# Attention and gated feed-forward on one core: TensorE's order from a written-out plan, and tanh tiles in a ring of eight gate pairs

## The chip, the core and the metric

The kernel runs on one core of a Trainium2 chip. The metric is the device time of one execution in microseconds (us); where several executions were timed, the median stands first and the range behind it. Four compute engines matter: TensorE (PE, matrix products), VectorE (DVE), ScalarE (ACT) and GpSimd (POOL). SyncE (SP) issues DMA transposes here, and GpSimd issues loads and stores. In the traces here each engine takes its instructions in the order of its stream: a copy on ScalarE whose input was complete at 328.97 us starts only at 329.69, behind two tanhs (shown below). The profile also gives the clock that TensorE was granted, as a share of full speed.

## The reference

```python
def _attn_ref(x, inducing):                  # x (4, 12416, 128), inducing (32, 128)
    ...
    def mab(q, kv):
        s = scale * (q @ kv.transpose(0, 2, 1))
        ...                                  # softmax: a
        return a @ kv
    h = mab(I, x)                            # 32 rows for each batch
    return mab(x, h)

def _moe_ref(x, w_gate, w_val, w_out):       # 49664 tokens, d_model 128, d_ff 1536
    gate = 1.0 / (1.0 + np.exp(-(x @ w_gate)))
    val = x @ w_val
    return gate * val @ w_out
```

The second attention multiplies weights `a` (tokens x 32) with `h` (32 x 128), and the feed-forward part multiplies that with `w_gate` and `w_val`. The kernel forms `h @ w_gate` and `h @ w_val` once for each batch, so gate and value need only a product over 32 rows for each token. The sigmoid is (1 + tanh(g/2))/2; the half is applied at the output.

## The kernel before

After a first stage (attention of batch 0) the work is 96 blocks of 512 tokens and a last, mixed one. `d_ff` is 12 chunks of 128. A block has four steps; each step multiplies a wide slot (two chunks, PSUM slot `a`) and a narrow slot (one chunk, PSUM slot `b`) on DVE. ScalarE makes tanh of gate *pairs* (two chunks), TensorE fills the slots and adds up the 12 output products in one PSUM tile, `acc`.

```python
    # buffers
    ps_g ... bufs=2   # gate pairs, and jobs      ps_a, ps_b ... bufs=1   # value slots
    ps_o ... bufs=1   # acc
    tp = ctx.enter_context(tc.tile_pool(name="tp", bufs=2))     # tanh: two whole blocks
    ...
    def g_tanh(bi, p, ps):
        if p == 0:
            Ts[bi] = tp.tile([P, NJ, TOK], F16, tag="T", name=f"T_{bi}")
        nc.scalar.activation(out=Ts[bi][:, 2 * p:2 * p + 2, 0:T], in_=..., func=AF.Tanh, scale=0.5)

    def v_mul(ps, bi, j0, n):                                   # (tanh + 1) * value
        u = up.tile([P, n, TOK], F16, tag=f"u{n}", name=f"u_{bi}_{j0}")
        nc.vector.scalar_tensor_tensor(
            out=u[:, :, 0:T], in0=Ts[bi][:, j0:j0 + n, 0:T], scalar=1.0, in1=...,
            op0=ALU.add, op1=ALU.mult)
        ...

    def out_store(bi):
        ...
        nc.scalar.activation(out=oT[:], in_=accs[bi][:], func=AF.Copy, scale=0.5)   # frees acc
        nc.sync.dma_start(on[:], oT[:], transpose=True)
        nc.gpsimd.dma_start(out[...], on[:])

    # the loop that sets the order
    for n in range(NBK):
        for k in range(4):
            for f in ev.get((n, k), ()):     # loads, transposes, sums of this half step
                f()
            ...
            v_fill(ps, n, 3 * k, 2)          # wide values
            for _ in range(min(pairs, gwant - gdone)):
                g_next()                     # gate pair right behind them
            ua = v_mul(ps, n, 3 * k, 2)
            outs(c0)                         # output matmuls of earlier chunks
            v_fill(ps, n, 3 * k + 2, 1)      # narrow value
            if k == 2 and n in extra:
                post = do_extra(*extra[n])   # a job; the step then does one output matmul less
            elif gdone < gwant:
                g_next(k == 3)
            ub = v_mul(ps, n, 3 * k + 2, 1)
            outs(c1)
```

Meanwhile the next batch's first attention is prepared in *jobs*, one in each of 49 blocks: `s1` (scores of x against the inducing rows, read from `xT`, a DMA transpose of a loaded quarter `xq`), `h` (sums with the exponentials `a1n`, again through a DMA transpose) and others. Where the loads and transposes stand is a table in half blocks:

```python
            plan = (   # load, load, transpose, transpose, s1 job, transpose of the exponentials, h jobs
                ((1, 0), (2, 0), (2, 2), (3, 2), 4, (5, 2), (7, 9)),
                ((5, 0), (6, 0), (6, 2), (7, 2), 8, (9, 2), (12, 13)),
                ((8, 0), (9, 0), (9, 3), (10, 2), 11, (12, 2), (14, 15)),
            )
```

The softmax here doesn't subtract the row's maximum and nothing guards it: scores larger than these inputs give would overflow.

## Time and profile before

| | before |
|---|---|
| time, median (range) | 746.33 us (743.2 to 750.3), 3 runs |
| span of the profiled execution | 739.6 us, granted clock 0.996 |
| busy: PE / DVE / ACT | 654.1 / 705.9 / 646.0 us |
| first to last multiply on DVE | 29.79 to 733.84 us |
| time in it in which DVE does nothing | 9.7 us |

How to read it: DVE is the full engine, so the time can only change by what DVE does or by how long it stands idle. I call "gaps" the time from the start of one DVE instruction to the start of the next, less the 1.14 us (wide) or 0.62 us (narrow) that it needs. The chain that ended last says the same: it is made mostly of DVE, with some TensorE. Shares of the span by engine, before:

```profile
DVE 61%; PE 24%; DMA 6%; ACT 5%; issue 3%; SPq 1%; POOL 0%; ACTq 0%; DVEq 0%; POOLq 0%
```

### The profile page before, as it was taken

The page shows a single profiled execution, that of the slowest core. Times are in us where ns is not written, and L with a number is a line of the kernel's source. Part 1 is how long each engine was busy: PE and PEld are TensorE (multiplying, and loading weights), DVE is VectorE, ACT ScalarE, POOL GpSimd, SP SyncE. Part 2 cuts the span into 40 slices and gives each one's busy share as a digit, 9 for nine tenths or more (in the row PEclk, how much of TensorE's full clock was granted, in tenths as well). Part 3 has the DMA queues.
Part 4 walks back from the last instruction along what each step waited for, and adds up shares of the span by engine and source line. Part 5 has one row for each costly group of instructions (what it writes and reads, how often), then busy time and mean ns, then how long its engine had stood idle before and what let it go on. Part 6 is the DMA issues. An engine that isn't in the chain of part 4 may idle for free.

```text
span 739.6 us, 12305 instructions
## 1 busy us (share of the span) xinstructions
PE 654.1 (88%) x4561; PEld 240.0 (32%) x4561; DVE 705.9 (95%) x838; ACT 646.0 (87%) x727; POOL 210.0 (28%) x317
## 2 busy tenths in 40 slices
PE   7888999989889889989889899998988988888886
PEld 4422333333232333333333233333323333233234
DVE  2599999999999999999999999999999999999997
ACT  4698899899889989889889899989988998988985
POOL 5234314303412512501611511430440241250000
PEclk9999999999999999999999999999999999999999
DMA  9569995523549799532448799562352343253222
GB/s 177 86 98 159 198 193 113 108 57 77 109 75 165 135 184 173 106 74 59 93 94 136 106 200 183 114 116 48 74 106 59 79 92 79 65 106 59 64 58 59
DMA packets 181900, 80.12 MB, mean 108 GB/s; under 512 B 165424, under 2 KB 166096, under 8 KB 181840
## 3 DMA queue, kind: packets, MB, share of 16 engines
q1 hardware_dynamic: 161856, 40.18, 32.9%
q0 software_dynamic: 19696, 39.03, 24.6%
q8 instruction: 35, 0.57, 0.3%
q14 instruction: 25, 0.20, 0.1%
q10 hardware_dynamic: 288, 0.13, 0.1%
HBM read 27.80 MB, written 25.43 MB: 72 GB/s over the span
## 4 chain that ended last, share of the span: by engine, by line
DVE 61%; PE 24%; DMA 6%; ACT 5%; issue 3%; SPq 1%; POOL 0%; ACTq 0%; DVEq 0%; POOLq 0%
DMA xq_4_127<-in_x_dram 2%; DMA xT_151<-xq_1_5310 1%; DMA xT_149<-xq_1_849 1%; DMA xT_149<-xq_3_1228 1%; ACT T_5362 L430 1%; DMA xT_151<-xq_3_5688 1%; DMA xT_150<-xq_3_3458 1%; ACT T_654 L430 1%; ACT T_3590 L430 0%; ACT T_8031 L430 0%; ACT T_7940 L430 0%; SPq L294 0%; ACT T_5820 L430 0%; ACT xT_148 L514 0%; PE acc_694 L472 0%
## 5 line engine op out<-in xcount | busy, mean ns | idle before, releaser
L472 PEld LDWEIGHTS <-wo_112 128*128 128x128 f16 x1152 | 103.4, 96 | 151.7 <-issue 80.8
L375 PEld LDWEIGHTS <-hw_163 32*128 32x128 f16 x432 | 16.5, 91 | 59.9 <-issue 56.9
L375 PEld LDWEIGHTS <-hw_160 32*128 32x128 f16 x434 | 16.4, 91 | 54.4 <-issue 51.0
L375 PEld LDWEIGHTS <-hw_161 32*128 32x128 f16 x432 | 16.3, 91 | 51.7 <-issue 48.2
L375 PEld LDWEIGHTS <-hw_162 32*128 32x128 f16 x432 | 16.2, 91 | 51.7 <-issue 48.2
L375 PEld LDWEIGHTS <-hwp_165 128*128 128x128 f16 x144 | 14.0, 97 | 21.3 <-issue 16.0
L375 PEld LDWEIGHTS <-hwp_166 128*128 128x128 f16 x144 | 13.9, 97 | 21.3 <-issue 15.6
L375 PEld LDWEIGHTS <-hwp_164 128*128 128x128 f16 x142 | 13.8, 97 | 20.9 <-issue 15.3
L375 PEld LDWEIGHTS <-hwp_167 128*128 128x128 f16 x144 | 13.9, 97 | 19.9 <-issue 14.3
L203 PEld LDWEIGHTS <-ones 128*128 128x128 f16 x96 | 7.0, 96 | 5.2 <-issue 3.5
L148 PE MATMUL warm<-ones 128*128 128x512 f16 x16 | 6.0, 558 | 1.5 <-DVE ones L98 1.5
L197 ACT ACTIVATE a1nt_200<-s1t_198 128x32 f16<-128x32 f32 x1 | 0.2, 197 | 6.3 <-PE s1t_198 L193 6.3
L691 PEld LDWEIGHTS <-indT 128*32 128x32 f16 x72 | 1.5, 93 | 9.9 <-issue 9.9
L483 ACT ACTIVATE o_9543<-acc_9458 128x256 f32<-128x256 f32 x2 | 0.8, 383 | 4.4 <-PE acc_9458 L462 3.9
L525 DVE COPY indT<-indT 128x32 f16<-128x32 f16 x1 | 0.2, 175 | 4.6 <-PE indT L524 4.6
L148 PEld LDWEIGHTS <-ones 128*128 128x128 f16 x23 | 2.7, 127 | 5.2 <-issue 3.0
L268 POOL COPY hwp_164<-hw_160 32x128 f16<-32x128 f16 x2 | 0.6, 283 | 13.3 <-ACT hw_160 L261 13.3
L329 POOL TENSOR_TENSOR a_0_2_0_1890<-e2n_2_1725,rc_2_1888 128x512 f16<-128x512 f16 x4 | 4.1, 1037 | 0.7 <-DVE rc_2_1888 L319 0.7
L329 POOL TENSOR_TENSOR a_2_2_0_6350<-e2n_2_6185,rc_2_6348 128x512 f16<-128x512 f16 x4 | 4.1, 1036 | 0.8 <-DVE rc_2_6348 L319 0.8
L329 POOL TENSOR_TENSOR a_1_2_0_4120<-e2n_2_3955,rc_2_4118 128x512 f16<-128x512 f16 x4 | 4.1, 1036 | 0.7 <-DVE rc_2_4118 L319 0.7
L329 POOL TENSOR_TENSOR a_3_1_0_7780<-e2n_1_7649,rc_1_7778 128x512 f16<-128x512 f16 x4 | 4.1, 1037 | 0.5 <-DVE rc_1_7778 L319 0.5
L329 POOL TENSOR_TENSOR a_2_0_0_4880<-e2n_0_4749,rc_0_4878 128x512 f16<-128x512 f16 x4 | 4.1, 1036 | 0.5 <-DVE rc_0_4878 L319 0.5
(4143 smaller groups left out, 2691.4 us busy)
## 6 DMA issues: line engine op xcount, KB each, us to landing
xq_0_115<-in_x_dram POOLq DMA_DIRECT2D x1, 512.0 KB, 5.2
xq_1_117<-in_x_dram POOLq DMA_DIRECT2D x1, 512.0 KB, 7.0
xq_2_123<-in_x_dram POOLq DMA_DIRECT2D x1, 512.0 KB, 8.4
xq_3_125<-in_x_dram POOLq DMA_DIRECT2D x1, 512.0 KB, 10.3
xq_4_127<-in_x_dram POOLq DMA_DIRECT2D x1, 512.0 KB, 13.9
xq_5_129<-in_x_dram POOLq DMA_DIRECT2D x2, 256.0 KB, 14.3
xq_0_758<-in_x_dram POOLq DMA_DIRECT2D x1, 512.0 KB, 6.8
xq_1_849<-in_x_dram POOLq DMA_DIRECT2D x1, 512.0 KB, 6.4
```

Source lines behind the costliest of these rows:

```text
L148: nc.tensor.matmul(ps[:, 0:TOK], ones[:, 0:P], ones[:], start=True, stop=True)
L197: nc.scalar.activation(out=an[:], in_=ps[:, 0:M], func=AF.Exp, scale=SCALE)
L203: nc.tensor.matmul(ps[:, cs:cs + P], ones[:, 0:P], a1n[(b, q)][:, j, :], start=first and j == 0, stop=last and j == 3,)
L268: nc.gpsimd.tensor_copy(out=pads[b][rows, 2 * i + jj, :], in_=hws[b][rows, p, :])
L329: nc.gpsimd.tensor_tensor(out=a2[:, r], in0=e2n[:, i, :, r, :].unsqueeze(2).to_broadcast((P, 4, 4, M)), in1=rc[:, i, :, r].unsqueeze(2).un ...
L375: nc.tensor.matmul(ps[:, ds(col, TOK)], weights(k["b"]), rep[rows, 4 * k["i"] + k["r"]], start=True, stop=True,)
L430: nc.scalar.activation(out=Ts[bi][:, 2 * p:2 * p + 2, 0:T], in_=ps[:].rearrange("p (a t) -> p a t", a=2)[:, :, 0:T], func=AF.Tanh, scale=0.5,)
L472: nc.tensor.matmul(accs[bi][:, 0:T], wo16[:, j, :], u, start=(c == 0), stop=(c == NJ - 1))
L483: nc.scalar.activation(out=o32[:, h:h + w, :].rearrange("p b c -> p (b c)"), in_=accs[bi][:, ds(h * P, w * P)], func=AF.Copy, scale=0.5,)
L525: nc.vector.tensor_copy(out=indT[:], in_=v[:, 0:M])
L691: nc.tensor.matmul(ps[r * M:(r + 1) * M, ts(i, TOK)], indT[:], xTs[a[0]][:, ds(q * QT + r * TOK, TOK)], start=True, stop=True,)
```

## The change

The intent is that TensorE's order is written out, letter by letter, instead of following from a loop. In a word of the plan (one word is a block) `A` fills and multiplies the wide slot of the next step, `B` the narrow one, `G` or `W` fills the next gate pair (`W` with weights that are padded with zeros to all 128 rows), `J` is the next job, and `a` to `l` are output matmuls. The tanh tiles become single pairs in a ring of eight. In odd steps the wide slot takes the last two of its three chunks and the narrow slot the first, so that a wide multiply reads exactly one pair. `PADV` names the chunks whose value weights are padded in the same way; it follows the new order of chunks. A block's store is issued when the next block has had six of its output matmuls.

```diff
+PLAN = (
+    "GAGBWGAabGBcGAfeGBdGAhBWgJ AGilkjBGGAabcBGAfGBedGAhGgBiG ..."
+    ...                                     # 97 words
-    tp = ctx.enter_context(tc.tile_pool(name="tp", bufs=2))
+    tp = ctx.enter_context(tc.tile_pool(name="tp", bufs=8))
-    PADG, PADV = (2,), (2, 5, 8, 11)
+    PADG, PADV = (2,), (2, 3, 8, 9)
 ...
-        if p == 0:
-            Ts[bi] = tp.tile([P, NJ, TOK], F16, tag="T", name=f"T_{bi}")
+        Ts[(bi, p)] = tp.tile([P, 2, TOK], F16, tag="T", name=f"T_{bi}_{p}")
 ...
-        nc.gpsimd.dma_start(out[...], on[:])
+        def store():
+            nc.gpsimd.dma_start(out[...], on[:])
+        stores.append(store)
 ...
+    def chunks(k):
+        return (3 * k, 3 * k + 2) if k % 2 == 0 else (3 * k + 1, 3 * k)
 ...                                         # the loop over n, k is replaced by:
+    for n, word in enumerate(words):
+        for c in word:
+            if c == "A":
+                ...                          # events of the step; v_fill and v_mul, wide
+            elif c == "B":
+                ...                          # v_fill and v_mul, narrow
+            elif c in "GW":
+                next_slot(c == "W")
+            elif c == "J":
+                post = do_extra(*jobs.popleft()[1])
+                if post:
+                    post()
+            else:
+                out_one(cur, ord(c) - ord("a"))
```

(A path that multiplies on GpSimd is in the diff too, but it is never taken.)

## The prediction

> **What bounds the kernel now.** I began with the page's busy shares.
>
> ```profile
> PE 654.1 (88%) x4561; PEld 240.0 (32%) x4561; DVE 705.9 (95%) x838; ACT 646.0 (87%) x727; POOL 210.0 (28%) x317
> ```
>
> The span is 739.6 us. VectorE (DVE) is busy for 705.9 of them, TensorE (PE) and ScalarE (ACT) for under 90%. The slices show that it is one stage and not an average over several.
>
> ```profile
> DVE  2599999999999999999999999999999999999997
> ACT  4698899899889989889889899989988998988985
> POOL 5234314303412512501611511430440241250000
> PEclk9999999999999999999999999999999999999999
> ```
>
> DVE is full from the third slice to the last but one. So the question is how much of its time is not work. I listed all DVE instructions in order of time; this is one block of 512 tokens from the middle.
>
> ```profile
> 346.30 1.22 DVE L443 SCALAR_TENSOR_TENSOR u_0_4734<-T_4686,va_0_4727 128x1024 f16<-128x1024 f16 x1
> 347.44 0.68 DVE L443 SCALAR_TENSOR_TENSOR u_2_4740<-T_4686,vb_0_4738 128x512 f16<-128x512 f16 x1
> 348.05 1.22 DVE L443 SCALAR_TENSOR_TENSOR u_3_4762<-T_4686,va_1_4751 128x1024 f16<-128x1024 f16 x1
> 349.19 0.68 DVE L443 SCALAR_TENSOR_TENSOR u_5_4766<-T_4686,vb_1_4764 128x512 f16<-128x512 f16 x1
> ```
>
> Columns: start, duration, engine, line. Durations overlap by 0.06 to 0.08 us, so I use start to start: 1.14 us from a wide multiply (two chunks of d_ff) to the next, 0.62 us from a narrow one (one chunk). A step is one of each, 1.76 us; a block is four steps, 7.04 us. There are 96 full blocks and a mixed one of the same shape: 388 wide and 388 narrow multiplies. The first starts at 29.79, the last at 733.84, 704.05 us apart. 388 x 1.14 + 387 x 0.62 = 682.2 us of that is multiplies. The excess over these pitches, added over the whole list (with 0.1 to 0.5 us allowed after each small DVE operation, as its own closest follower shows), is 9.7 us; the other 12 us are the small operations themselves. Before 29.79 lies the first attention stage, after the last multiply the output tail of 5.7 us.
>
> Of the 9.7 us, 2.3 lie in block 0 and at the start of block 1. About 4.8 lie behind the nine "s1" jobs (scores of the next batch), which sit in TensorE's in-order stream and wait for a DMA transpose of x. The worst:
>
> ```profile
> PE s_2_3702 L691 <- DMA xT_150<-xq_3_3458: 1.4, 1, 1.4
> PE s_3_5552 L691 <- DMA xT_151<-xq_1_5310: 1.0, 1, 1.0
> PE s_1_1092 L691 <- DMA xT_149<-xq_1_849: 1.0, 1, 1.0
> PE s_3_5932 L691 <- DMA xT_151<-xq_3_5688: 0.8, 1, 0.8
> ```
>
> This is the view of TensorE's waits (total, times, longest, in us). While it stands there it fills no value slot and DVE starves; after the first of these DVE begins its next multiply 1.6 us late, at 271.01. The remaining 2.6 us are lags of under 0.1 us, mostly at a block's first multiply.
>
> **What the Trainium skill says.** "Perfetto Trace Analysis", section Identifying the Most-Contended Engine, takes occupancy as a fair measure for VectorE, but not matmul busy time for TensorE: I trust the 95% and not the 88%. "VectorE: DVE Perf Modes", section Why PSUM operands drop a tier, caps an fp32 PSUM operand at the plain mode of one element a cycle; at the 0.96 GHz of its Specifications 1024 elements are 1.07 us (an estimate from that page) and the trace has 1.14, so the multiply has no slack. Its section The DRAIN you can't avoid found that a semaphore between DVE operations costs nothing extra; here the narrow multiplies with one kind of wait start on average 1.134 us after the wide ones, those with two 1.139, so it agrees. "TensorE: Matmul & The Clock Gate", section The mechanism (packing), says that matmuls on different row groups overlap. The trace agrees: a value pair (rows 64 to 127) and the gate pair after it (rows 0 to 63) start 0.01 us apart, 347.57 and 347.58.
>
> **The change part by part.** I compared the two programs instruction by instruction. TensorE has 9112 of them in both, DVE 840, ScalarE 731, GpSimd 254 and SyncE 172. Nothing is removed or added: the GpSimd multiply path in the diff is dead, because the set of shared blocks is empty. DVE's 388 + 388 multiplies keep their shapes. So 682 + 12 us of DVE work stay, and only the 9.7 us of gaps, the head and the tail can move.
>
> (1) Chunk order in odd steps. A wide multiply now takes exactly one gate pair. Same count and width: 0 us. It lets tanh tiles be rings of pairs.
>
> (2) Ring of eight pairs instead of two whole blocks. Counting the plan, at the first multiply of a step 6 or 7 gate pairs have been issued beyond the one needed (300 of 388 steps), where the old loop ran about 3 or 4 ahead. That takes ScalarE's latency off the path, but in the old trace DVE waited for a tanh only 1.0 us, once, at the very start. Worth under 0.5 us. More multiplies now carry a ScalarE wait: 0 us by the semaphore numbers above.
>
> (3) TensorE order. Before, the gate pair stood right behind the value pair and ran beside it. In the plan the token ahead of a value pair is a gate pair in 320 of 388 steps, and what follows it is mostly output matmuls. Matmuls of 512 columns go every 0.215 us, and each change between row-packed and full matmuls costs about 0.1 us (308.88 to 309.21 for two packed pairs). A block is 12 output matmuls, 4 full value ones, 2 full gate ones, 4 value pairs and 5 packed gate pairs. If each pair runs alone that is 27 x 0.215 = 5.8 us, and with some 12 changes 7.0 us, against 7.04 on DVE. Where the value pair needs not wait, gate and value overlap and it is nearer 6 us. So TensorE stays barely below DVE. Before, a packed value pair had waited for DVE by 0.2 to 0.4 us in many steps; the margin shrinks but I expect it to hold. The small lags are 2.6 us: I take off 1.5.
>
> (4) The head. The plan interleaves gates, values and the first query job at block 0's end. The 2.3 us may shrink to about 1, but the job now stands directly before the DVE reduction that reads it, which can cost some 0.7 again: take off 1.
>
> (5) Jobs and stores. The s1 job moves from the third step of its block to the second, about 1.8 us earlier, for all nine. Alone that would deepen the six waits in the first two rounds by as much: +8 or more. Against it, the HBM store of a block is now issued half a block later, so GpSimd no longer stops for the output transpose (waits of 5 to 10 us stood in its queue) ahead of loading x and scaling the attention weights; the loads and transposes behind it come earlier, I guess by 1 to 2 us. The plan puts h jobs at different steps in different batches (first, second, third step for the first one of the three), which looks fitted to landing times seen on a chip; I therefore let the two cancel with a small gain: take off 1.5.
>
> Sum: 0.5 + 1.5 + 1 + 1.5 = 4.5 us. Taken from the timed median of 746.3 (the profiled execution was 741.3, so timed runs carry about 5 us more, which I leave in), that is 742.
>
> **The rivals.** *A. All gaps go:* -9.7 us, 736 or so. For it: DVE is full otherwise and the plan looks tuned. Even this is 1.3%, so 2% is out of reach unless the timed runs' extra 5 us are gaps too. *B. The earlier s1 jobs stall TensorE:* 1.8 us for six to nine jobs, +8 to +14 us after what is saved elsewhere, 752 to 758. For it: five of nine already wait for the transpose, or for what follows from it, and a transpose takes 5 to 6 us from issue to landing whatever the order is. Against: the cleared GpSimd queue. *C. TensorE becomes the bound:* with 7.0 us plus about 1 us in each of 49 blocks with a job, up to 0.5 us per such block, +20 us, 765. Against it: pairs overlap as soon as TensorE is late, which corrects itself.
>
> **Range and chances.** The floor from DVE's work is about 735, so the low end is 735. The upper end takes in most of B: 752. Faster by over 2% needs 731.4, below the floor: 0.04. Slower by over 2% needs 761.3, which only C or B with more gives: 0.06.
>
> **What would show it.** Right: DVE still at 1.14 and 0.62, its busy time within 2 us of 706, the four waits of TensorE for x's transposes about as long or shorter, the first multiply still near 29.8, GpSimd's waits for the output transposes mostly gone. Wrong: a wide multiply that regularly starts over 1.8 us after the one before (C), waits of 2 to 4 us of TensorE for the transposes of x (B), or a first wide multiply much earlier than 29.8.

## The result, and the profile after

| | before | after |
|---|---|---|
| time, median (range) | 748.32 us (743.2 to 752.55), 4 runs | 774.67 us (770.03 to 777.02), 4 runs |
| profiled span, granted clock | 739.6 us, 0.996 | 775.2 us, 0.982 |
| first to last multiply on DVE | 29.79 to 733.84 us | 29.87 to 769.82 us |
| gaps in it | 9.7 us | 45.7 us |

The ratio is 1.0348, with a 95% interval of 1.0262 to 1.0433: slower, outside the predicted range of 735 to 752. Ratios in this text are the mean time of one kernel's fast runs over the mean of the other's in the same rounds, so they are not quite the ratio of the medians. The four before lie within 1.3% of each other. The two profiled spans lie 35.6 us apart and the medians 26.4, because the profiled run before was a short one (741.32 us, below all four of the table) and the one after the longest of its four.

The page after, busy shares:

```profile
PE 713.8 (92%) x4561; PEld 248.6 (32%) x4561; DVE 712.4 (92%) x838; ACT 641.9 (83%) x727; POOL 208.9 (27%) x317
```

and its slices of a fortieth of the span:

```profile
DVE  2699499999999979999999798999999999999997
ACT  4799389889889879888888787988988898888883
PEclk9999699999999989999999899999999999999999
```

DVE has the same 838 instructions. It is busy 6.5 us longer (712.4 against 705.9 us), but the durations of all its instructions add up to the same, 760.4 against 760.2 us: neighbours that follow each other directly overlap a little, and those with a gap between them do not. Its fifth slice now holds a hole (4), two further slices are at 7 and one at 8 (the last slice was at 7 before, too). In the fifth slice the granted clock falls too (6). TensorE is busy 60 us longer with the same 4561 matmuls. That alone is no loss (run e9 below has 710.2 us of it and is not slower): where two packed matmuls used to run beside each other they now run one after the other, as part (3) of the prediction counted. The chain that ended last has turned over, from DVE to TensorE:

```profile
PE 49%; DVE 26%; ACT 10%; DMA 7%; issue 6%; SPq 1%; POOL 0%; ACTq 0%; DVEq 0%; POOLq 0%
```

I sorted the gaps by size. Those of 0.6 us and more grew from 5.6 to 24.4 us (nine of them), those of 0.1 to 0.6 us from 1.4 us (four) to 16.2 us (sixty), those below 0.1 us from 2.7 to 5.1 us. So there are two different losses of about the same size: a few long stops, and a small loss in every other block. Together they make the 36.0 us by which the gaps grew, and the time from first to last multiply grew by 35.9.

**The few long stops.** TensorE's waits after (total, times, longest, in us):

```profile
PE h_1387 L244 <- DMA a1n_0_1232<-e_1_0_1112: 9.1, 1, 9.1
PE s_3_6213 L751 <- DMA xT_154<-xq_3_5989: 2.7, 1, 2.7
PE s_3_5813 L751 <- DMA xT_154<-xq_1_5590: 2.5, 1, 2.5
PE s_2_3863 L751 <- DMA xT_153<-xq_3_3639: 2.3, 1, 2.3
...
PE s_2_3463 L751 <- DMA xT_153<-xq_1_3240: 0.5, 1, 0.5
```

The four waits of `s1` jobs for a transpose of x, which were 4.2 us together, are 8.0. And a wait stands there that the kernel before did not have: the `h` job of block 7 waits 9.1 us for the transposed exponentials. The plan has this job in the first step of its block, two steps (3.5 us) earlier than the old loop; the rest is that the transpose landed late. SyncE's queue shows the issue of that transpose:

```profile
73.01 5.49 SPq L220 DMA_TRANSPOSE a1n_0_1232<-e_1_0_1112  x1
```

and TensorE's timeline its end:

```profile
93.35 0.29 PE L244 MATMUL h_1387<-a1n_0_1232,ones 128*128 128x128 f16 x1 [9.14 <-DMA a1n_0_1232<-e_1_0_1112]
```

The transpose needed 20.3 us from issue to landing. In the kernel before the same transpose was issued at 78.03 and needed 6.9. In the stretch between, 85 to 90 us, the DMA engines were busy but moved only 72 GB/s, and no compute engine did anything. The table by windows has the columns window, length, then busy us (and instructions) of PE, PEld, DVE, ACT and POOL, then the granted clock, the DMA share as the view counts it, and GB/s:

```profile
85.00:90.00 5.00, 0.00 (x0) 0.00 (x0) 0.00 (x1) 0.00 (x0) 0.00 (x0) 0.50 1.42 72
...
281.00:284.00 3.00, 0.74 (x8) 0.11 (x3) 1.23 (x2) 1.12 (x2) 1.07 (x2) 0.82 1.18 213
284.00:290.00 6.00, 6.00 (x24) 1.27 (x20) 3.38 (x4) 3.97 (x4) 1.06 (x2) 0.52 1.00 167
```

The last two lines show what a stop costs beyond itself. In 281 to 284 TensorE waits the 2.3 us for x's transpose. In the six us after it TensorE is busy all the time, but at half its clock (0.52), and a matmul of 512 columns lasts 0.61 instead of 0.39 us; DVE is busy only 3.38 of six us. DVE's gaps between 281 and 291 us come to 5.0 us, over twice the wait. The trace has a control for this. In the stop that ends at 471.8 us TensorE waited 2.7 us, but the clock stayed at 1.00, and DVE's gaps there come to 2.8 us, about the wait itself:

```profile
469.00:472.00 3.00, 0.30 (x8) 0.10 (x3) 1.12 (x1) 0.92 (x2) 1.06 (x2) 1.00 1.26 234
472.00:478.00 6.00, 5.96 (x40) 2.13 (x36) 5.20 (x6) 5.21 (x6) 1.04 (x2) 1.00 0.70 104
```

So, as far as one trace shows, a stop with the half clock costs DVE some 2.5 us on top of the wait. (The third stop, 434 to 437, has 5.1 us of gaps for a wait of 2.5; 0.9 of them stand behind a reciprocal, as they do before the change.) In the kernel before, the longest such wait was 1.4 us, and the clock stayed:

```profile
268.00:270.00 2.00, 0.60 (x9) 0.21 (x8) 1.47 (x2) 0.73 (x1) 1.06 (x2) 1.00 0.99 222
270.00:275.00 5.00, 4.81 (x32) 1.62 (x29) 3.97 (x5) 4.67 (x6) 0.86 (x2) 1.00 0.84 154
```

**The small loss.** A piece of the timeline from the middle, where no transfer is waited for (start, duration, engine, line; in brackets the idle time before and what ended it):

```profile
327.86 1.02 ACT L470 ACTIVATE T_0_4465<-g_0_4462 128x1024 f16<-128x1024 f32 x1 [0.79 <-DVE u_10_4453 L483]
...
328.78 1.02 ACT L470 ACTIVATE T_1_4472<-g_1_4469 128x1024 f16<-128x1024 f32 x1
...
329.69 0.60 ACT L548 ACTIVATE oT_4483<-acc_4394 128x512 f16<-128x512 f32 x1
...
330.34 0.59 PE L526 MATMUL acc_4501<-u_0_4478,wo_115 128*128 128x512 f16 x2 [0.36 <-ACT oT_4483 L548]
...
331.23 0.68 DVE L483 SCALAR_TENSOR_TENSOR u_3_4506<-T_1_4359,vb_1_4504 128x512 f16<-128x512 f16 x1
...
331.73 0.39 PE L416 MATMUL va_2_4519<-rep_1_3562,hw_164 32*128 32x512 f16 x2
...
332.27 1.22 DVE L483 SCALAR_TENSOR_TENSOR u_6_4522<-T_3_4403,va_2_4519 128x1024 f16<-128x1024 f16 x1 [0.36 <-PE va_2_4519 L416]
```

Read it from the top. ScalarE has a gate pair ready but stands 0.79 us, until the multiply `u_10` has read its tanh: all eight pairs of the ring are taken. Then come that tanh and the next one, and only behind them, at 329.69, the copy `oT` that empties the output accumulator, although its last matmul had ended near 328.97. There is one accumulator, so TensorE's first output matmul of the next block waits 0.36 us for that copy, at the head of an in-order stream. The wide values behind it start at 331.73, and DVE begins `u_6` 1.04 us after `u_3` where 0.62 would do: 0.42 us lost. The waits added up over the whole trace fit this: ScalarE's tanh for a multiply of DVE 37.1 us in 81 waits (before, practically none), TensorE's `acc` for `oT` 17.7 us in 50.

### The profile page after: what moved, and what is told of

Same layout as the page of the kernel before. It is cut to its first block, busy times and chain, and to the rows that moved or that the text cites.

```text
span 775.2 us, 12803 instructions
## 1 busy us (share of the span) xinstructions
PE 713.8 (92%) x4561; PEld 248.6 (32%) x4561; DVE 712.4 (92%) x838; ACT 641.9 (83%) x727; POOL 208.9 (27%) x317
## 4 chain that ended last, share of the span: by engine, by line
PE 49%; DVE 26%; ACT 10%; DMA 7%; issue 6%; SPq 1%; POOL 0%; ACTq 0%; DVEq 0%; POOLq 0%
DMA a1n_0_1232<-e_1_0_1112 3%; DMA xq_4_130<-in_x_dram 2%; DMA xT_154<-xq_1_5590 1%; DMA xT_153<-xq_1_3240 1%; DMA xT_153<-xq_3_3639 1%; DMA xT_154<-xq_3_5989 1%; PE acc_5824 L526 1%; PE acc_3874 L526 1%; PE acc_4501 L526 0%; PE acc_8977 L526 0%; PE acc_9230 L526 0%; PE acc_1730 L526 0%; PE acc_5527 L526 0%; PE acc_4607 L526 0%; PE acc_4394 L526 0%
## 5 line engine op out<-in xcount | busy, mean ns | idle before, releaser
L526 PEld LDWEIGHTS <-wo_115 128*128 128x128 f16 x1152 | 90.4, 97 | 167.3 <-issue 128.4
L416 PEld LDWEIGHTS <-hw_166 32*128 32x128 f16 x432 | 19.4, 91 | 61.9 <-issue 60.8
L416 PEld LDWEIGHTS <-hw_165 32*128 32x128 f16 x432 | 19.2, 91 | 59.9 <-issue 58.4
L416 PEld LDWEIGHTS <-hw_163 32*128 32x128 f16 x434 | 19.1, 91 | 59.5 <-issue 56.2
L416 PEld LDWEIGHTS <-hw_164 32*128 32x128 f16 x432 | 19.0, 91 | 56.5 <-issue 54.9
L416 PEld LDWEIGHTS <-hwp_170 128*128 128x128 f16 x144 | 14.0, 97 | 17.4 <-issue 4.3
L416 PEld LDWEIGHTS <-hwp_168 128*128 128x128 f16 x144 | 14.2, 99 | 16.3 <-issue 3.2
L416 PEld LDWEIGHTS <-hwp_167 128*128 128x128 f16 x142 | 13.9, 98 | 17.1 <-issue 5.4
L416 PEld LDWEIGHTS <-hwp_169 128*128 128x128 f16 x144 | 14.1, 98 | 15.5 <-issue 3.6
L554 POOL DMA_DIRECT2D out_dram<-on_1291 x1 | 0.5, 532 | 19.9 <-DMA on_1291<-oT_1289 19.9
L370 POOL TENSOR_TENSOR a_2_1_0_5862<-e2n_1_5705,rc_1_5860 128x512 f16<-128x512 f16 x4 | 4.1, 1037 | 3.7 <-DVE rc_1_5860 L360 3.7
L370 POOL TENSOR_TENSOR a_0_1_0_1150<-e2n_1_1000,rc_1_1148 128x512 f16<-128x512 f16 x4 | 4.1, 1037 | 2.5 <-DVE rc_1_1148 L360 2.5
```

Of the source, the lines that this page charges most:

```text
L370: nc.gpsimd.tensor_tensor(out=a2[:, r], in0=e2n[:, i, :, r, :].unsqueeze(2).to_broadcast((P, 4, 4, M)), in1=rc[:, i, :, r].unsqueeze(2).un ...
L416: nc.tensor.matmul(ps[:, ds(col, TOK)], weights(k["b"]), rep[rows, 4 * k["i"] + k["r"]], start=True, stop=True,)
L526: nc.tensor.matmul(accs[bi][:, 0:T], wo16[:, j, :], u, start=(c == 0), stop=(c == NJ - 1))
L554: nc.gpsimd.dma_start(out[ds(row0, QT)].rearrange("(p j) c -> p j c", j=QT // P)[:, 4 * k["r"]:4 * k["r"] + 4, :], on[:],)
```

## The experiments

The theory after reading the two traces: (R) the ring of eight is full, since the plan runs six or seven pairs ahead, and the small loss follows from that; (D) `s1` and `h` jobs stand earlier than their transfers can land, and the long stops follow from that. Rivals: TensorE's new order itself is too tight; the late stores disturb the transfers; the output matmuls stand too early. Twelve kernels were run, all compared with the kernel before on the same chip. All gave results that the comparison with the reference accepted. The medians and ranges in the table include the slow runs (one of e11, three of e12); the ratios leave them out.

Two cautions. Differences from the changed kernel (774.67 us) are between medians of different rounds, some on other chips. Taken from the ratios instead, e5 gains 1.5, e7 2.0 and e9 4.4 points on it, which is about 11, 15 and 33 us, each uncertain by about 8 us. And the gaps of the experiments are counted as the time from first to last multiply less 694.3 us, which is what remains of it without the gaps in both profiles above.

| run | median us (range) | ratio to before (95%) |
|---|---|---|
| after, e1: old order | 741.23 (740.47 to 744.84) | 0.9969 (0.9908 to 1.0031) |
| e2: jobs moved back | 775.90 (774.65 to 785.40) | 1.0453 (1.0368 to 1.0539) |
| e3: stores at once | 776.68 (774.38 to 781.20) | 1.0426 (1.0352 to 1.0500) |
| before, e4: jobs early | 796.24 (794.92 to 798.52) | 1.0702 (1.0639 to 1.0766) |
| e5: ring of twelve | 758.91 (755.33 to 762.10) | 1.0199 (1.0131 to 1.0267) |
| e6: outputs later | 771.49 (769.13 to 774.57) | 1.0371 (1.0305 to 1.0438) |
| e7: data ready | 755.63 (754.83 to 764.24) | 1.0150 (1.0081 to 1.0219) |
| e8: old order, two jobs later | 743.08 (741.21 to 747.27) | 0.9997 (0.9945 to 1.0050) |
| e9: ring of twelve and data ready | 741.09 (738.42 to 743.14) | 0.9909 (0.9870 to 0.9948) |
| e10: ring of twelve, jobs back | 761.43 (759.81 to 763.41) | 1.0179 (1.0139 to 1.0220) |
| e11: ring of twelve, jobs last | 767.41 (765.10 to 780.32) | 1.0255 (1.0206 to 1.0304) |
| e12: ring of twelve, x earlier | 740.95 (734.88 to 752.81), 22 runs | 0.9926 (0.9899 to 0.9953) |

### e1: the old order in the new kernel

The plan is replaced by words written from the old loop, everything else of the change stays: ring of eight, chunk order, late stores, padded chunks.

```diff
-  ... AlkBjWAbaBGGAcfBedGAghBGi ...      # block 20
+  ... AGklBjAGGBabcAGeBfdAGgBWhi ...
-  ... AlkjBWAJbBaGAcBfGeGAdhBgiG ...     # block 8, with a job
+  ... AGikBljAGGBabcAGeBJfAGdBWgh ...
```

> The changed kernel with one edit: the plan string is generated from the loop of the kernel before (same order of gates, values, outputs and jobs), while the ring of eight, the chunk order of odd steps, the padded chunks and the late stores stay. My theory: all of the loss (36 us between the two profiles) comes from the order of TensorE, so this runs within 1% of the kernel before, 742 to 754 us, and VectorE's gaps fall from 45.7 us to 8 to 14. Rival 1 (the late stores crowd the DMA queues): still a wait of over 5 us for a transpose in block 7 and 755 to 765 us. Rival 2 (ring or chunk order cost something by themselves): gaps of 0.1 to 0.5 us spread over all blocks, over 755 us.

Measured 741.23 us against 743.66 for before in the same rounds: the same time. Gaps on DVE 10.1 us, against 9.7. TensorE's longest waits for DVE and for x's transposes:

```profile
PE va L403 <- DVE u L470: 58.4, 204, 0.6
PE s L738 <- DMA xT<-xq: 2.1, 2, 1.1
```

TensorE waits for DVE again, which is how it should be when DVE is the bound. So nothing in the change costs time but the order; or rather, the ring, the chunk order and the late stores cost nothing *under the old order*, which runs only about three pairs ahead.

### e2: the jobs moved back behind the narrow chunk of the third step

```diff
-  AlkjBWAJbBaGAcBfGeGAdhBgiG             # block 8
+  AlkjBWAbBaGAcBJfGeGAdhBgiG
```

(31 words change: all those whose job stood earlier.)

> The changed kernel with only the jobs that the plan had moved ahead put back behind the narrow value chunk of the third step, as before. My theory: of the 36 us about 23 are job waits (12.9 at the h job of block 7, about 10 more than before at the s1 jobs), the other 13 small lags by the order. So the s1 waits fall back to 1.0 to 1.4 us each and the time to 752 to 760 us; about 13 us of lags stay. If the transpose that the h job of block 7 waits for still lands as late as 93 us, 4 to 5 us of its wait stay and the time is at the upper end. Rival (job positions do not matter, the transposes are late because of the stores): 768 or more.

Measured 775.9 us. This expectation missed. The waits of `s1` and `h` jobs for transposes are gone but for 0.2 us, and the granted clock is 0.997, but the gaps are still 43.8 us: 25 gaps of 0.55 us and more, up to 1.3 us, stand directly behind jobs (6 in the changed kernel), and the small loss is as large as before. TensorE's and ScalarE's waits:

```profile
PE acc L513 <- ACT oT L535: 20.8, 60, 0.7
...
ACT T L457 <- DVE u L470: 37.7, 84, 0.9
```

So the waits for transfers are not the whole loss, and where a job stands in this plan has a price of its own.

### e3: the stores issued at once, as before

```diff
-        stores.append(store)
+        store()
```

> The changed kernel with the store of each block issued at once again, as in the kernel before, nothing else. Rival 1 (late stores let two loads of x and two stores start beside the transposes at 70 to 76 us, and the transpose a1n of block 7 lands 20 us after its issue instead of 7): a1n lands in 7 to 10 us, the wait of 9.1 us goes, 760 to 766 us. My theory has no strong view of this term; if the DMA crowding comes from the earlier jobs and not from the stores, the wait stays over 5 us and the time within 1% of 775.

Measured 776.68 us, not faster. The `h` wait is shorter and the waits for x's transposes twice as long:

```profile
PE acc L526 <- ACT oT L548: 17.0, 50, 0.4
PE s L751 <- DMA xT<-xq: 15.6, 7, 3.7
...
PE h L244 <- DMA a1n<-e: 4.6, 1, 4.6
```

The late stores are not the cause. With them the `s1` jobs waited 7.6 us less and the `h` job 4.5 us more, in one profiled execution each. If they help, as the prediction guessed, it is by little, and the times do not tell the two kernels apart.

### e4: the kernel before, with its jobs one step earlier

```diff
-            if k == 2 and n in extra:
+            if k == 1 and n in extra:
```

> The kernel before with one edit: every job runs in the second step of its block instead of the third, the rest of the order untouched. My theory: TensorE's waits for transposes of x grow from 0.8 to 1.4 us to 2 to 3 us in the four to six s1 jobs, and its clock is halved after the longest of them, so 8 to 20 us slower than before, 756 to 768. Rival (job position is harmless, only the small lags of the order count): within 0.5% of before.

Measured 796.24 us, far more than expected. Two things happen:

```profile
PE s L691 <- DMA xT<-xq: 12.6, 6, 6.9
PE h L203 <- ACT T L430: 10.3, 18, 0.6
```

The waits for transposes triple against 4.2 us, which shows that the position of the `s1` jobs matters by itself, in the old order too. But about 43 gaps of 0.6 us and more stand behind nearly every job. In the old loop the second step has just filled two gate pairs, which is all the slots that gates and jobs share; a job moved there waits until ScalarE has read one of them (the second line, 0.6 us each), and the next values stand behind it. So this run is not a clean measure of D: most of its loss is one of the old loop's own.

### e5: a ring of twelve pairs

```diff
-    tp = ctx.enter_context(tc.tile_pool(name="tp", bufs=8))
+    tp = ctx.enter_context(tc.tile_pool(name="tp", bufs=12))
```

> The changed kernel with the ring of tanh tiles at twelve pairs instead of eight, nothing else. In the changed kernel's trace ScalarE waits 37 us (81 times) for VectorE to free a tanh tile, so the copy of the finished output accumulator queues behind late tanhs, and TensorE's first output matmul of a block waits 17.7 us (50 times, up to 0.4) for that copy. My theory now: the ring is the cause of these lags. With twelve, ScalarE's waits for VectorE go to under 5 us, the accumulator waits to under 6 us, VectorE's gaps of 0.1 to 0.6 us from 16 us to under 8, and the time falls by 8 to 13 us to 760 to 767. Rival (the outputs simply come too early in the plan whatever the ring): accumulator waits stay at 12 us or more and the time within 1% of 775.

Measured 758.91 us, 15.8 below the changed kernel. Twelve pairs of 2 KB a partition are what the two whole blocks of the kernel before took. Waits of TensorE and ScalarE:

```profile
PE h L244 <- DMA a1n<-e: 8.9, 1, 8.9
...
PE s L751 <- DMA xT<-xq: 7.6, 4, 2.9
...
ACT T L470 <- DVE u L483: 3.4, 5, 1.0
```

ScalarE's 37.1 us of waits for a free pair are 3.4, `acc` waits for `oT` 1.1 us in place of 17.7, and the gaps fall from 45.7 to 29.9 us. The gaps of 0.1 to 0.6 us are about 5 us in 14, where they were 16.2 in sixty. The long stops are where they were (22.7 us, against 24.4). This shows R.

### e6: three output matmuls later

In 87 of the 97 blocks the first outputs of a block are moved out of the second step behind its narrow chunk, so that `oT` has more time.

```diff
-  AGlkjBWAbBGacGAfeBGdAhBGgiG            # block 21
+  AGlkjBWABbGacGAfeBGdAhBGgiG
```

> The changed kernel with the block's own first outputs (a, b, c) in the second step moved from before the narrow value chunk to right behind it, in 87 of 97 blocks; gates, jobs and all else as they are. Theory of the accumulator: TensorE's waits for the accumulator's copy fall from 17.7 us to under 4 and the time by 8 to 13 us, to 762 to 768. Rival (the lags come from too many switches between packed and full matmuls, TensorE being short of time): the waits vanish but the gaps stay, and the time is within 1% of 775.

Measured 771.49 us, hardly below the changed kernel. The waits of `acc` are gone, but ScalarE's waits for the ring stay (35.4 us in 79), and some 11 of the 16.2 us of small gaps stay (47 of sixty). The likely reason is that the outputs now stand in front of the next wide values; no run tests it. The wait for `oT` is a link of the chain, not its cause; taking out the link leaves most of the delay.

### e7: jobs that read data that lies ready

Wrong on purpose: the `s1` job reads the batch before's transposed x, and the `h` job the exponentials of batch 0. Same instructions, other addresses, and all transfers still run. (The comparison with the reference passed all the same; its tolerance does not see this.)

```diff
-                        xTs[a[0]][:, ds(q * QT + r * TOK, TOK)], start=True, stop=True,
+                        xTs[a[0] - 1][:, ds(q * QT + r * TOK, TOK)], start=True, stop=True,
...
+            held_a1 = a1n[(a[0], a[1])]
+            a1n[(a[0], a[1])] = a1n[(0, NQ - 1)]
             h_mm(ps, *a, True, True, a[1] == 0)
+            a1n[(a[0], a[1])] = held_a1
```

> Wrong result on purpose: the changed kernel, in which the score jobs read the transposed x of the batch in work and the h jobs read attention weights of batch 0, both long there; the same instructions in the same order, the same DMAs. It takes away only the waits of TensorE for transposes in flight. Theory: the waits of 9.1 and 8.0 us go, and with them the halved clock after each; of the 36 us that the change cost, 20 to 24 come back, 750 to 756 us. The 17 us of accumulator waits stay. Rival (the lags absorb it, or other waits take their place): 763 or more.

Measured 755.63 us, 19.0 below the changed kernel. The waits of `s1` and `h` are gone, and the small loss is untouched (`acc` waits 16.5 us in 49). The profiled execution was the longest of the five, 764.24 us, with one stop of 5.3 us on a late sum of GpSimd at 130 us; the other four were within 754.83 to 757.32, at granted clocks of 0.997 to 0.999, against 0.982 to 0.989 of the changed kernel. This shows D, and that the lower clock came with the stops.

### e9: both

Edit: e5 and e7 together, wrong like e7.

> Wrong result on purpose: e5 and e7 together, a ring of twelve and jobs that read data long there, in the plan of the changed kernel. If the full ring and the waits for transposes are two separate causes, their gains add: e5 took 16 us and e7 19 us off the changed kernel's 775, so 738 to 746 us, within 1% of the kernel before, with VectorE's gaps at 8 to 14 us. If TensorE is also short of time in this order, 750 or more remain.

Measured 741.09 us. The two gains were 15.8 and 19.0 us alone, 34.8 together, and both at once gave 33.6. By the ratios it is 11 and 15 us alone and 33 at once, so that they add up is shown only to within some 10 us. The gaps of the profiles point the same way: 15.8 us fewer in e5, 12.9 in e7 (18.2 without its late sum), 38.2 here. What e9 shows for certain is that the two causes together leave nothing of the loss. The page of this run:

```profile
PE 710.2 (96%) x4561; PEld 244.1 (33%) x4561; DVE 705.3 (96%) x838; ACT 639.1 (87%) x727; POOL 208.9 (28%) x317
```

TensorE is as busy as DVE, 96%, and the gaps are 7.5 us. The rival that the order itself is too tight falls, as far as all tiles and data are there.

### e10 and e11: the ring of twelve, and jobs later, with right results

e10 is e5 with the words of e2; in e11 the jobs stand behind the narrow chunk of the last step.

```diff
-  AlkjBWAJbBaGAcBfGeGAdhBgiG             # block 8
+  AlkjBWAbBaGAcBJfGeGAdhBgiG             # e10
+  AlkjBWAbBaGAcBfGeGAdhBJgiG             # e11
```

> A right result: the ring of twelve of e5 and the jobs back in the third step as in e2. In e2 the waits for transposes were gone but the time was not, at 776 us, with more accumulator waits (20.8 us) and gaps of 0.6 to 0.7 us behind 20 jobs. If those too came from the full ring, 742 to 750 us here. If TensorE has no room for a job at that place in the plan (the old order left out a gate there, the plan does not), the gaps of 0.6 behind the jobs stay, about 12 us, and it is 755 to 762.

> As e10, with the jobs behind the narrow chunk of the fourth step, where every transpose has landed. No waits for transposes. With room for the jobs: 738 to 746 us, which would equal or beat both kernels. Without room: as e10, 755 to 762.

Measured 761.43 and 767.41 us: e10 is the same as e5 within the noise (1.0179 and 1.0199), e11 rather slower (1.0255). Next to no transfer is waited for (in e10 0.5 us at an `s1` job and 2.2 us at a gate, in e11 none) and the clock is full, but 22 and 32 gaps of 0.55 us and more stand directly behind jobs (5 in e5). One of them in e10:

```profile
89.44 1.22 DVE L470 SCALAR_TENSOR_TENSOR u<-T,va 128x1024 f16<-128x1024 f16 x1 [0.58 <-ACT T L457]
```

The plan had put jobs into steps with fewer other matmuls: in block 8 the second step has two outputs and one gate besides the job, where block 21 has three outputs and two gates. The reading is that TensorE, 96% busy in this order (e9), has no room for a job elsewhere; this is inferred from where the gaps stand. (The old loop made room by one output matmul less, not by a gate, as the expectation of e10 has it.) So the jobs were not simply misplaced: in this plan they have to stand early, and then their data must come earlier.

### e8: the old order with two score jobs at the end of their blocks

This tried to beat the kernel before from its own side: the words of e1, the first word of the new plan, and the `s1` jobs of blocks 4 and 8 of each batch (counted from 0) later in the block.

```diff
-  AGikBljAGGBabcAGeBJfAGdBWgh            # block 8, in the words of e1
+  AGikBljAGGBabcAGeBfAGdBJWgh
```

> A try to beat both kernels: the changed kernel with the old order of e1, but the first block's word from the new plan (2.9 us of gaps in block 0 become about 1.1) and the score jobs of the first two rounds at the end of their block, one step later than before, where the transposes have landed (2.2 us of gaps in e1, 4.8 in the kernel before). Expected: gaps of VectorE of 8.4 us in e1 fall to 4 to 6, 736 to 741 us, 0.5 to 1% faster than the kernel before. If the late jobs delay the chain behind them, it is not faster.

Measured 743.08 us, ratio 0.9997. No gain. The profiled execution, the longest of the six, had a wait of 4.1 us for a transpose of x; the others have no trace.

### e12: the ring of twelve, and x loaded earlier

The plan stays as it is. Loads and transposes of the next batch's x are issued one block earlier, two of the three transposes of the exponentials half a block earlier.

```diff
-                ((1, 0), (2, 0), (2, 2), (3, 2), 4, (5, 2), (7, 9)),
-                ((5, 0), (6, 0), (6, 2), (7, 2), 8, (9, 2), (12, 13)),
-                ((8, 0), (9, 0), (9, 3), (10, 2), 11, (12, 2), (14, 15)),
+                ((0, 0), (1, 0), (1, 2), (2, 2), 4, (5, 0), (7, 9)),
+                ((4, 0), (5, 0), (5, 2), (6, 2), 8, (9, 0), (12, 13)),
+                ((7, 0), (8, 0), (8, 3), (9, 2), 11, (12, 2), (14, 15)),
```

> A right result, meant to reach e9: the changed plan with its jobs where they are and a ring of twelve, and instead of later jobs earlier data. The loads of the next batch's x and their transposes are issued one block (7 us) earlier, the transposes of the attention weights for the h jobs half a block earlier. TensorE waited 2.3 to 2.9 us for these transposes and 9 us at the h job, so most of it should be covered: 742 to 750 us, against 759 for e5. If the added DMAs only crowd each other (the h job's transpose took 20 us from issue to landing in a crowded stretch), a wait of 5 us or more stays somewhere and it is 752 to 760.

Measured 740.95 us in 22 runs, against 745.28 in 27 runs of the kernel before: ratio 0.9926, so 0.7% below the kernel before and 4.4% below the changed one (740.95 / 774.67), with a right result. The 0.7% is clear of the noise but under 2%. Part of it is that 11 of the 26 fast runs of the kernel before had a granted clock under 0.992 and took 749.3 us on average; of the 19 fast runs of e12 one had (742.9 us). Among the other fast runs the means are 740.3 and 743.0 us. In the profiled run no `s1` or `h` job waits for a transfer and the gaps are 10.6 us; the largest is 3.7 us, ending at 259.9, a gate waiting for its attention weights:

```profile
PE g L416 <- DMA rep<-a: 3.6, 2, 3.0
```

## Why the prediction was wrong

The prediction was 742 us within 735 to 752; it came to 774.67. The right parts first.

**What bounds the kernel.** Right: DVE's multiplies kept their pitches of 1.14 and 0.62 us, nothing was removed or added, and only the gaps moved. That is why the loss could be counted in them. (The prediction's average starts, 1.134 and 1.139 us, compare one kind of wait with two; they do not show what a wait costs against none.)

**(1) Chunk order.** Right, 0 us: e1 has it and takes the time of before.

**(4) The head.** Right in size: the gaps in block 0 and at the start of block 1 fell from 2.3 to about 1.1 us, and the first multiply stayed at 29.87 against 29.79.

**(2) The ring of eight. This step failed.** It read "where the old loop ran about 3 or 4 ahead. That takes ScalarE's latency off the path" and booked a gain of under 0.5 us. The count of six or seven pairs ahead was right, and it was the warning: with the pair in use, seven ahead fill a ring of eight. From then on a tanh starts only when DVE gives a pair back, and ScalarE's in-order stream holds everything behind it, the copy that frees the only accumulator above all. The cost was 15.8 us (e5; about 11 by the ratios), not a gain of 0.5. The Trainium skill has this in "Perfetto Trace Analysis", section Optimization Strategy: the same gap repeating on the engine that should be full can mean that there is no memory for the next tile. The trace agrees: sixty gaps of 0.1 to 0.6 us, and four more buffers take most of them away.

**(3) TensorE's order.** The working was right as far as it went: TensorE's busy time rose to 710 to 714 us, matmul pairs run one after another, and still it does not set the time (e9, where it is as busy as DVE, 96%). Rival C, TensorE as the bound at 765 us, is not what happened, although its sign came: of some 355 steps without another operation in them, 91 took over 1.8 us from one wide multiply to the next, where 26 did before. With the ring of twelve and ready data (e9) it is 40, so most of this was the full ring. But "the margin shrinks but I expect it to hold" holds only if no wait falls into it: with no slack, 0.36 us of waiting reaches DVE, and a job moved out of its place costs about 0.6 us (e10, e11). The gain of 1.5 us from small lags is not shown by any run: e9 has 2.2 us less of gaps than the kernel before, but its jobs wait for no transpose, and in the kernel before those waits cost about 4.8.

**(5) Jobs and stores. This step failed too.** "I therefore let the two cancel with a small gain: take off 1.5" was the choice against Rival B. The deepening by earlier `s1` jobs came as B had it, and with it B's sign, waits of 2 to 4 us (2.3, 2.5 and 2.7); but it was smaller than B's sum (waits 4.2 to 8.0 us in all; 15.6 in e3, with the stores at once). What no rival had was the `h` job of block 7, alone 9.1 us, and the half clock that follows some of the stops. Together the stops cost 19.0 us (e7; about 15 by the ratios), against +8 to +14 of B. B's premise, that a transpose takes 5 to 6 us "whatever the order is", held for x (medians of 5.0 to 5.4 us after, 5.3 to 6.1 before) and failed for the exponentials of block 7 (20.3 us). The argument that different steps for `h` jobs look "fitted to landing times seen on a chip" was not evidence from a view. The expected sign, that GpSimd's waits for output transposes would mostly go, did not come either: they add up to 483 us in 80 waits, where they were 468 in 95. The longest, in the stop of block 7, is 19.9 us, where it was 10.8 before:

```profile
L554 POOL DMA_DIRECT2D out_dram<-on_1291 x1 | 0.5, 532 | 19.9 <-DMA on_1291<-oT_1289 19.9
```

**The range.** The chance of slower by over 2% was put at 0.06, because the rivals were treated one at a time. Two failures that add, each near 2%, were not among them.

**What stays open.** Why the transpose of the exponentials for block 7 took 20.3 us is not settled. A load of x (17.4 us to landing) and a store (15.7 us) overlapped it and were slow as well, and the stop came back at the same place in e5 and e6 (8.9 and 8.3 us), at 4.6 us in e3, and not in e1, e2 and e12. It goes with the early jobs and the place of the loads; which of the transfers holds up which no run here isolates.

## What to carry to other kernels

When a plan runs further ahead, count the buffers that the lead needs, with the tile in use and the one being written, before counting what the lead hides: a full ring makes an engine off the critical path wait, and whatever stands behind it in its stream waits too. When in-order work is moved earlier, move the transfers that it reads by as much in the same edit; here four more buffers and loads one block earlier turned a loss of 3.5% into a gain of 0.7%. And when an order uses up the slack of a second engine, ask for each small wait of it where it now ends up.

## What the Trainium skill lacked or had wrong

- "TensorE: Matmul & The Clock Gate", section HAM oscillation, gives the rule that no idle gap of TensorE should exceed about 3.4 us. Here shorter waits sufficed: after a wait of 2.3 us the granted clock was 0.52 for six us (284 to 290), after one of 2.5 us 0.50 (437 to 443). After a longer one of 2.7 us, ending at 471.8, it stayed at 1.00, so the length of the wait alone does not decide it. Waits for transposes of up to 1.4 us (profile of the kernel before) did not show it.
- The same page has no figure for what such a drop costs another engine that TensorE feeds: DVE's gaps around the wait of 2.3 us come to 5.0 us, roughly twice its length, and around the wait of 2.7 us at full clock to 2.8.
- "DMA: Bandwidth & Descriptors" would be the place for the latency of a DMA transpose beside other traffic; it gives a bandwidth for transposes, but I found no such latency there. One transpose of 128 x 1024 f16 took 6.9 us from issue to landing in one order of the program, and 20.3 us in the other.
